# Bucketed attention and a gated Fourier projection on one core: interleaving the two, keeping x on chip, and rewriting four inner pieces

## The chip, the cores and the metric

The kernel runs on one core of one Trainium2 chip. The metric is the device time of one execution in microseconds (us). TensorE is called PE below, VectorE DVE, ScalarE ACT, GpSimd POOL and SyncE SP, as the profile calls them. One run of the kernel before (902.01 us) was slow, and the ratios leave it out. A ratio is the mean time of one kernel's fast runs over that of the other's fast runs of the same rounds, so it is not quite the ratio of the medians that are quoted.

Some terms. PSUM is the memory that matmuls write to, in banks; copying a result out of it is an eviction. A lone pair is a pair of heads in attention that runs with no projection beside it. DFT is the Fourier transform as a product with a table.

## The reference, cut to what matters

Four batches, eight heads, 768 positions, 64 values per head. A query sees only the keys whose six sign bits equal its own. The result, as a matrix x of 768 x 512 per batch, is projected to x1, x2 and x3; x2 is convolved with a filter by way of a Fourier transform, the three are multiplied, and the product is projected again.

```python
q_bits = (einsum('bhsd,dk->bhsk', q, proj) > 0)          # 6 bits; k_bits likewise
mask = q_bucket[:, :, :, None] == k_bucket[:, :, None, :]
scores = where(mask, scale * q @ k.T, -1e9)
attn = exp(scores - max); attn = attn / (sum(attn) + 1e-9)
x = (attn @ v) -> (batch, seq, 512)

x1, x2, x3 = split(x @ w_proj, 3)                        # w_proj 512 x 1536
x2_conv = irfft(rfft(x2) * rfft(filter_fft))             # over the 768 positions
out = (x1 * x2_conv * x3) @ w_out
```

## The kernel before

It does all attention first, sends x to DRAM, then loads tables and weights, then does four projections. In attention the bucket match is a 64-wide table row: signs `hh`, a matmul with a code table (`yps`), two passes of ACT, and the result lies as rows 64 to 127 beside q and k.

```python
tz = ...; zps = matmul(projpad, tz)                       # sign projections, fp32
nc.vector.tensor_scalar(hh[0:70, :], zps[0:70, :], 0.0, None, ALU.is_gt)
nc.tensor.matmul(yps[0:64, 0:512], code_sb[0:6, :], hh[0:6, 0:512])   # ... 4 of them
nc.scalar.activation(prA[HD:P, :], yps[0:HD, :], AF.Relu, bias=..., scale=sc)
...
for jt in range(NCH):                                     # head_front
    stp = pp.tile([P, SEQ], FP32, tag="ps", name="stp")   # two matmuls, then
    nc.scalar.activation(ptj, stp, AF.Exp, bias=negbump_sb, scale=1.0)
...                                                       # pv: 14 matmuls
nc.scalar.copy(t32, pv[0:HD, :])
nc.vector.tensor_tensor(t32, t32, pv[HD:P, :], ALU.add)
nc.vector.tensor_copy(lall[k32 : k32 + 1, :], pv[96:97, :])   # one head's divisors
...
nc.vector.reciprocal(rall, lall)                          # once per four heads
... rhia, rloa = high and low part; rb = matmul(sel128_sb, rhia) + ...  # broadcast
nc.vector.tensor_tensor(u32, t32, rb[0:HD, :], ALU.mult)  # head_tail
... xthi, xtlo -> DRAM
```

The projection works through PSUM tiles of four two-bank buffers, with the forward and inverse transform as plain products with 768 x 768 tables (six row blocks each):

```python
for it in range(NCH): ppj = 12 matmuls; nc.vector.tensor_copy(x2t, ppj)
for jp in range(3):   ab = 2 x 6 matmuls with wfh; 4 products and 2 sums on DVE
for ct in range(NF):  cpd = 2 x 6 matmuls with ivh; p1, p3 = 48 matmuls; 3 DVE operations
for tt_ in range(NCH): op_ = 8 matmuls; nc.vector.tensor_scalar_mul(osb, op_, 1.0 / YSCALE)
```

The softmax here doesn't subtract the row's maximum and nothing guards it: scores larger than these inputs give would overflow.

Of the kernel before, what the change touches and what calls it, by code (L numbers as in the profile page):

```python
# [12 lines left out]
BF16 = mybir.dt.bfloat16  # L14
# [3 lines left out]
P = 128  # L18
SEQ = 768
HD = 64  # L20
NCH = SEQ // P
MASK_BUMP = 30.25
DELTA = 1.0e-7
YSCALE = 1024.0

SPLIT_WPROJ = True
SPLIT_FWD = False
SPLIT_INV = False
SPLIT_WOUT = True
SPLIT_HDFT = True  # L30


def _dft_basis():
    N = SEQ
    tt, rr = np.meshgrid(
        np.arange(N, dtype=np.float64), np.arange(N, dtype=np.float64), indexing="ij"
    )
    kk = np.where(rr <= N // 2, rr, rr - N // 2)
    ang = 2.0 * np.pi * tt * kk / N
    return np.where(rr <= N // 2, np.cos(ang), np.sin(ang))  # L40


def _bucket_consts():
    c = np.arange(64)
    bits = ((c[None, :] >> np.arange(6)[:, None]) & 1).astype(np.float64)
    return 2.0 * bits - 1.0, bits.sum(0)


def _hilo(x):
    hi = x.astype(np.float16)  # L50
    lo = (x - hi.astype(np.float64)).astype(np.float16)
    return hi, lo


@with_exitstack
def kernel(
# [17 lines left out]
    WF64 = _dft_basis()  # L74
    wf_hi, wf_lo = _hilo(WF64)
    wft_hi, wft_lo = _hilo(np.ascontiguousarray(WF64.T))
    wfhi_d = nc.inline_tensor(wf_hi, name="wfhi")
    wflo_d = nc.inline_tensor(wf_lo, name="wflo")
    wfthi_d = nc.inline_tensor(wft_hi, name="wfthi")
    wftlo_d = nc.inline_tensor(wft_lo, name="wftlo")  # L80
    eye_dram = nc.inline_tensor(np.eye(P, dtype=np.float32), name="eye128")

    code_np, pc_np = _bucket_consts()
    code_t = np.zeros((P, 64), dtype=np.float16)
    code_t[0:6, :] = code_np
    code_t[64:70, :] = code_np
    code_dram = nc.inline_tensor(code_t, name="ohcode")
    bias_q = np.zeros((P, 1), dtype=np.float32)
    bias_q[0:64, 0] = MASK_BUMP * (1.0 - pc_np)
    bias_q[64:128, 0] = MASK_BUMP * (1.0 - pc_np)  # L90
    bias_k = np.zeros((P, 1), dtype=np.float32)
    bias_k[0:64, 0] = 1.0 - pc_np
    bias_k[64:128, 0] = 1.0 - pc_np
    biasq_dram = nc.inline_tensor(bias_q, name="biasq")
    biask_dram = nc.inline_tensor(bias_k, name="biask")
    wcol = np.full((P, 3), 2.0 / SEQ, dtype=np.float32)
    wcol[0, 0] = 1.0 / SEQ
    wcol_dram = nc.inline_tensor(wcol, name="wcol")
    import ml_dtypes
    sel = np.zeros((P, 64), dtype=np.float64)  # L100
    sel[0::32, :] = 1.0
    sel128_dram = nc.inline_tensor(sel.astype(ml_dtypes.bfloat16), name="sel128")
    d32 = np.zeros((P, 1), dtype=np.float32)
    d32[32, 0] = 1.0
    d32_dram = nc.inline_tensor(d32, name="d32")

    cp = ctx.enter_context(tc.tile_pool(name="consts", bufs=1))
    pp = ctx.enter_context(tc.tile_pool(name="psm", bufs=4, space=bass.MemoryType.PSUM))
    drp = ctx.enter_context(tc.tile_pool(name="drs", bufs=1, space=bass.MemoryType.DRAM))

    ident = cp.tile([P, P], FP32, name="ident")
    nc.sync.dma_start(ident, eye_dram.ap())
    code_sb = cp.tile([P, 64], FP16, name="code_sb")
    nc.sync.dma_start(code_sb, code_dram.ap())
    biasq_sb = cp.tile([P, 1], FP32, name="biasq_sb")
    nc.sync.dma_start(biasq_sb, biasq_dram.ap())
    biask_sb = cp.tile([P, 1], FP32, name="biask_sb")
    nc.sync.dma_start(biask_sb, biask_dram.ap())
    wcol_sb = cp.tile([P, 3], FP32, name="wcol_sb")
    nc.sync.dma_start(wcol_sb, wcol_dram.ap())  # L120
    sel128_sb = cp.tile([P, 64], BF16, name="sel128_sb")
    nc.sync.dma_start(sel128_sb, sel128_dram.ap())
    projpad = cp.tile([P, 70], FP32, name="projpad")
    nc.vector.memset(projpad, 0.0)
    nc.sync.dma_start(projpad[0:HD, 0:6], proj)
    nc.sync.dma_start(projpad[HD:P, 64:70], proj)
    eps_sb = cp.tile([P, SEQ], BF16, name="eps_sb")
    nc.vector.memset(eps_sb, DELTA)
    negbump_sb = cp.tile([P, 1], FP32, name="negbump_sb")
    nc.vector.memset(negbump_sb, -MASK_BUMP)  # L130
    zero_sb = cp.tile([P, 1], FP32, name="zero_sb")
    nc.vector.memset(zero_sb, 0.0)
    d32_sb = cp.tile([P, 1], FP32, name="d32_sb")
    nc.sync.dma_start(d32_sb, d32_dram.ap())

    xhi_dr = drp.tile([NBAT, NF, P, SEQ], FP16, name="xhi_dr")
    xlo_dr = drp.tile([NBAT, NF, P, SEQ], FP16, name="xlo_dr")

    GRP = 4
    with (  # L140
        tc.tile_pool(name="prime", bufs=26) as prime_p,
        tc.tile_pool(name="qn", bufs=8) as qnp,
        tc.tile_pool(name="qz", bufs=2) as qzp,
        tc.tile_pool(name="hb", bufs=2) as hbp,
        tc.tile_pool(name="pt", bufs=19) as ptp,
        tc.tile_pool(name="vp", bufs=6) as vpp,
        tc.tile_pool(name="grp", bufs=3) as grpp,
        tc.tile_pool(name="ux", bufs=6) as uxp,
    ):
        qpr = {}  # L150
        kpr = {}

        def prep_chunk(b, pr, which):
            hA, hB = 2 * pr, 2 * pr + 1
            if True:
                tensor = q if which == "q" else k
                natA = qnp.tile([P, NCH, HD], FP32, tag="qn", name="natA")
                nc.sync.dma_start(
                    natA, tensor[b, hA].rearrange("(c p) d -> p c d", p=P)
                )  # L160
                natB = qnp.tile([P, NCH, HD], FP32, tag="qn", name="natB")
                nc.sync.dma_start(
                    natB, tensor[b, hB].rearrange("(c p) d -> p c d", p=P)
                )
                tpsA = pp.tile([HD, SEQ], FP32, tag="ps", name=f"tpsA_{which}")
                tpsB = pp.tile([HD, SEQ], FP32, tag="ps", name=f"tpsB_{which}")
                for c in range(NCH):
                    nc.tensor.transpose(tpsA[0:HD, ts(c, P)], natA[:, c, :], ident)  # L168
                    nc.tensor.transpose(tpsB[0:HD, ts(c, P)], natB[:, c, :], ident)
                tz = qzp.tile([P, SEQ], FP32, tag="qz", name="tz")  # L170
                nc.vector.tensor_copy(tz[0:HD, :], tpsA)  # L171
                nc.vector.tensor_copy(tz[HD:P, :], tpsB)  # L172
                prA = prime_p.tile([P, SEQ], FP16, tag="prime", name="prA")
                prB = prime_p.tile([P, SEQ], FP16, tag="prime", name="prB")
                scl = 0.125 if which == "q" else 1.0
                nc.scalar.mul(prA[0:HD, :], tpsA, scl)
                nc.scalar.mul(prB[0:HD, :], tpsB, scl)
                zps = pp.tile([70, SEQ], FP32, tag="ps", name=f"zps_{which}")
                nc.tensor.matmul(zps[:, 0:512], projpad, tz[:, 0:512])  # L179
                nc.tensor.matmul(zps[:, 512:SEQ], projpad, tz[:, 512:SEQ])  # L180
                hh = hbp.tile([P, SEQ], FP16, tag="hb", name="hh")
                nc.vector.tensor_scalar(hh[0:70, :], zps[0:70, :], 0.0, None, ALU.is_gt)  # L182
                yps = pp.tile([P, SEQ], FP32, tag="ps", name=f"yps_{which}")
                nc.tensor.matmul(yps[0:64, 0:512], code_sb[0:6, :], hh[0:6, 0:512])
                nc.tensor.matmul(yps[0:64, 512:SEQ], code_sb[0:6, :], hh[0:6, 512:SEQ])
                nc.tensor.matmul(yps[64:P, 0:512], code_sb[64:70, :], hh[64:70, 0:512])
                nc.tensor.matmul(  # L187
                    yps[64:P, 512:SEQ], code_sb[64:70, :], hh[64:70, 512:SEQ]
                )
                bias_sb = biasq_sb if which == "q" else biask_sb  # L190
                sc = MASK_BUMP if which == "q" else 1.0
                nc.scalar.activation(  # L192
                    prA[HD:P, :], yps[0:HD, :], AF.Relu, bias=bias_sb[0:HD], scale=sc
                )
                nc.scalar.activation(
                    prB[HD:P, :], yps[HD:P, :], AF.Relu, bias=bias_sb[HD:P], scale=sc
                )
                if which == "q":
                    qpr[(b, hA)], qpr[(b, hB)] = prA, prB
                else:  # L200
                    kpr[(b, hA)], kpr[(b, hB)] = prA, prB

        def v_prefetch(b, h):
# [10 lines left out]
            )  # L214
            return vpr

        def head_front(b, h, lall, vpr, filler=None):
            k32 = 32 * (h % GRP)
            ptl = []
            for jt in range(NCH):  # L220
# [311 lines left out]
```

## Time and profile before

| | before |
|---|---|
| median of 4 runs beside the changed kernel | 890.69 us (888.58 to 896.31) |
| attention (0 to 558 us), one pair of heads | 34.2 us (half of 68.3 us per four heads; 20.2 us in the last batch, which prepares no next q and k) |
| tables, weights, filter transform (558 to 594.7 us) | 36.7 us |
| projection, per batch | 72.9 us, four times |

First the page of the kernel before: busy time by engine, then tenths of busy time in 40 slices of the span (22.3 us each), and the granted PE clock in tenths.

```profile
span 891.1 us, 8416 instructions
PE 644.7 (72%) x3256; PEld 319.7 (36%) x3256; DVE 444.8 (50%) x515; ACT 294.7 (33%) x361; POOL 56.9 (6%) x138
...
PE   4666746746646747647647482299999999999997
...
POOL 0022002002002001001112000100000000000000
PEclk9989977976985985985998786599999999999999
...
```

The PE row splits in two. Up to slice 24 it is at 4 to 8 tenths, then at 2 for two slices (the end of attention, then the loading of tables); from slice 27 to 39 it stands at 9 (90% or more). POOL is nearly idle throughout. The view of windows gives the same in numbers; its columns are window, length, busy time of each engine with its instructions, mean granted clock, DMA share and GB/s. First four heads of attention, then one projection:

```profile
core 0: us, PE busy (x) PEld busy (x) DVE busy (x) ACT busy (x) POOL busy (x), PEclk, DMA share, GB/s
187.00:256.00 69.00, 41.70 (x200) 19.61 (x200) 37.53 (x41) 36.73 (x45) 6.55 (x16) 0.83 0.20 46
594.70:667.60 72.90, 72.90 (x398) 38.40 (x396) 36.20 (x51) 0.00 (x0) 0.00 (x0) 1.00 0.11 37
```

In 69 us of attention no engine is full (PE 41.7 us, DVE 37.5, ACT 36.7). In the projection PE is busy all 72.9 us at full clock. So it looks as if in attention engines wait for each other in turn. The chain of waits of the kernel before, in order of time (start, us, what), shows its longest link, once per four heads:

```profile
187.50 0.97 DVE lall L247
...
188.49 4.96 DVE rall L297
...
194.37 0.94 DVE rloa L301
...
195.35 0.64 PE rb L261 x2
...
200.35 1.00 DVE xtlo L275 x2
```

From `lall` to `xtlo` more than 13 us go by in which PE has under 2 us of the chain's work. In the groups (busy us, mean ns, idle before) the wide reciprocal and the one-row copy stand out:

```profile
L297 DVE RECIPROCAL rall<-lall 128x768 f32<-128x768 f32 x8 | 39.6, 4953 | 0.3
...
L247 DVE COPY lall<-pv 1x768 f32<-1x768 f32 x32 | 30.7, 961 | 0.4
```

The copy of one row of 768 values takes 961 ns. In the chain above, the last head's copy stands at its head, at 187.50.

### The profile page before, as it was taken

What the parts mean: (1) busy time and instruction counts of PE and PEld (TensorE: products, weight loads), DVE (VectorE), ACT (ScalarE), POOL (GpSimd) and SP (SyncE); (2) the same over time, 40 slices, a digit from 0 to 9 for tenths busy, and PEclk for the clock granted to TensorE, in tenths of its full rate; (3) what the DMA queues carried; (4) which work ended last, traced back from release to release, by engine and by line L of the source; (5) the groups of instructions that cost most, each with busy time, mean ns of one, the idle gap of its engine ahead of it and who ended that gap; (6) DMA issues with size and microseconds to landing.
All of it is one profiled execution on the core that took longest, in us unless ns stands there. A gap on an engine that the chain in (4) does not pass through costs nothing.

```text
span 891.1 us, 8416 instructions
## 1 busy us (share of the span) xinstructions
PE 644.7 (72%) x3256; PEld 319.7 (36%) x3256; DVE 444.8 (50%) x515; ACT 294.7 (33%) x361; POOL 56.9 (6%) x138
## 2 busy tenths in 40 slices
PE   4666746746646747647647482299999999999997
PEld 2333313313322323322323231044554554554553
DVE  3333465365465365456457657476334533623633
ACT  2447734734734744743756471000000000000000
POOL 0022002002002001001112000100000000000000
PEclk9989977976985985985998786599999999999999
DMA  5242103103102202202101016920030011001001
GB/s 102 57 94 62 34 17 78 42 18 80 45 18 71 54 18 71 54 18 71 36 1 36 1 35 210 288 99 0 1 118 24 1 48 60 1 1 71 1 1 71
DMA packets 94263, 46.92 MB, mean 53 GB/s; under 512 B 78736, under 2 KB 90128, under 8 KB 94224
## 3 DMA queue, kind: packets, MB, share of 16 engines
q1 hardware_dynamic: 93360, 45.60, 19.1%
q0 software_dynamic: 864, 0.79, 0.5%
q8 instruction: 26, 0.43, 0.2%
q14 instruction: 13, 0.11, 0.0%
HBM read 34.58 MB, written 12.58 MB: 53 GB/s over the span
## 4 chain that ended last, share of the span: by engine, by line
PE 58%; DVE 24%; ACT 7%; issue 6%; DMA 3%; SPq 1%; POOL 0%; POOLq 0%; ACTq 0%; DVEq 0%
PE pv L240 8%; PE x1ps L476 7%; PE x3ps L476 7%; PE wprojB L416 7%; ACT ptj L229 5%; DVE rall L297 4%; PE wout L496 4%; PE idft L458 4%; PE fdft L432 3%; DVE hh L182 3%; DVE tz L172 3%; DVE tz L171 3%; PE zps_q L179 3%; DVE xtlo L275 2%; PE zps_k L179 2%
## 5 line engine op out<-in xcount | busy, mean ns | idle before, releaser
L229 ACT ACTIVATE ptj<-stp,negbump_sb 128x768 f16<-128x768 f32 x192 | 158.2, 906 | 29.5 <-PE stp L225 27.9
L240 PE MATMUL pv<-ptj,vpr 128*128 128x256 f16 (+1 forms) x384 | 81.7, 353 | 0.4
L255 PE MATMUL rb<-rhia,sel_sb 32*64 32x512 bf16 (+1 forms) x64 | 15.2, 516 | 69.6 <-ACT rhia L299 69.6
L222 PE MATMUL stp<-prA 128*128 128x512 f16 x96 | 43.4, 464 | 18.8 <-ACT ptj L229 13.0
L240 PEld LDWEIGHTS <-vpr 128*128 128x128 f16 x384 | 40.1, 104 | 34.6 <-issue 13.3
L179 PE MATMUL zps_q<-tz,projpad 128*70 128x512 f32 x32 | 22.8, 802 | 37.8 <-DVE tz L172 37.8
L222 PE MATMUL stp<-prB 128*128 128x512 f16 x96 | 33.9, 378 | 18.1 <-ACT ptj L229 18.1
L297 DVE RECIPROCAL rall<-lall 128x768 f32<-128x768 f32 x8 | 39.6, 4953 | 0.3
L420 DVE CAST x2tile<-wprojB 128x512 f16<-128x512 f32 x24 | 16.5, 690 | 40.1 <-PE wprojB L416 40.1
L179 PE MATMUL zps_k<-tz,projpad 128*70 128x512 f32 x32 | 17.8, 639 | 23.3 <-DVE tz L172 23.3
L182 DVE TENSOR_SCALAR hh<-zps_q 70x768 f16<-70x768 f32 x16 | 15.3, 954 | 35.2 <-PE zps_q L180 35.2
L255 PEld LDWEIGHTS <-sel_sb 32*64 32x64 bf16 x64 | 4.7, 135 | 78.0 <-issue 78.0
L168 PE MATMUL tpsA_q<-ident,natA 128*64 128x128 f32 x96 | 24.6, 333 | 10.3 <-DMA natA<-in_q_dram 8.3
L225 PE MATMUL stp<-prA 128*128 128x256 f16 x96 | 31.9, 332 | 0.0
L247 DVE COPY lall<-pv 1x768 f32<-1x768 f32 x32 | 30.7, 961 | 0.4
L192 ACT ACTIVATE prA<-yps_q,biasq_sb 64x768 f16<-64x768 f32 x16 | 14.3, 894 | 49.0 <-PE yps_q L187 49.0
L171 DVE COPY tz<-tpsA_q 64x768 f32<-64x768 f32 x16 | 15.2, 948 | 29.0 <-PE tpsA_q L168 29.0
L171 DVE COPY tz<-tpsA_k 64x768 f32<-64x768 f32 x16 | 15.2, 950 | 28.5 <-PE tpsA_k L168 28.5
L182 DVE TENSOR_SCALAR hh<-zps_k 70x768 f16<-70x768 f32 x16 | 15.3, 954 | 27.7 <-PE zps_k L180 27.7
L192 ACT ACTIVATE prA<-yps_k,biask_sb 64x768 f16<-64x768 f32 x16 | 14.3, 894 | 39.4 <-PE yps_k L187 39.4
L500 DVE TENSOR_SCALAR osb<-wout 128x512 f32<-128x512 f32 x24 | 16.4, 692 | 21.1 <-DMA out_dram<-osb 10.8
L416 PEld LDWEIGHTS <-xh 128*128 128x128 f16 x192 | 18.8, 98 | 22.6
(622 smaller groups left out, 1514.5 us busy)
## 6 DMA issues: line engine op xcount, KB each, us to landing
out_dram<-osb SPq DMA_DIRECT2D x24, 256.0 KB, 2.1
natA<-in_q_dram SPq DMA_DIRECT2D x16, 192.0 KB, 2.5
natB<-in_q_dram SPq DMA_DIRECT2D x16, 192.0 KB, 2.7
natA<-in_k_dram SPq DMA_DIRECT2D x16, 192.0 KB, 2.7
natB<-in_k_dram SPq DMA_DIRECT2D x16, 192.0 KB, 2.8
xhi_dr<-xthi SPq DMA_DIRECT2D x32, 96.0 KB, 2.2
xlo_dr<-xtlo SPq DMA_DIRECT2D x32, 96.0 KB, 2.1
xh<-xhi_dr SPq DMA_DIRECT2D x16, 192.0 KB, 3.7
```

The source lines that it names most:

```text
L171: nc.vector.tensor_copy(tz[0:HD, :], tpsA)
L179: nc.tensor.matmul(zps[:, 0:512], projpad, tz[:, 0:512])
L182: nc.vector.tensor_scalar(hh[0:70, :], zps[0:70, :], 0.0, None, ALU.is_gt)
L222: nc.tensor.matmul(stp[:, 0:512], kpr[(b, h)][:, ts(jt, P)], qpr[(b, h)][:, 0:512])
L225: nc.tensor.matmul(stp[:, 512:SEQ], kpr[(b, h)][:, ts(jt, P)], qpr[(b, h)][:, 512:SEQ])
L229: nc.scalar.activation(ptj, stp, AF.Exp, bias=negbump_sb, scale=1.0)
L240: nc.tensor.matmul(pv[:, lo_c:hi_c], vpr[:, jc, :], ptl[jc][:, lo_c:hi_c], start=False, stop=(jc == NCH - 1),)
L297: nc.vector.reciprocal(rall, lall)
L416: nc.tensor.matmul(ppj, lh, rh, start=(i == 0), stop=(i == len(terms) - 1))
L458: nc.tensor.matmul(cpd[:, lo_c:hi_c], lh, rh, start=(i == 0), stop=(i == len(terms) - 1),)
L476: nc.tensor.matmul(dest[:, lo_c:hi_c], lh, rh, start=(i == 0), stop=(i == len(terms) - 1),)
L496: nc.tensor.matmul(op_, lh, rh, start=(i == 0), stop=(i == len(terms) - 1))
```

## The change

The intent: let PE do the projection of batch b while batch b+1 is in attention, so that neither half's waits leave PE idle, and shorten the attention chain. Its parts:

- **Order.** The loop runs the four pairs of batch b, then writes the projection of batch b-1; a scheduler decides the order on each engine. PSUM is split: 2 x 2 banks for scores, 2 for `pv`, 2 single banks (`psW`) for everything else.
- **x on chip.** The 16 pair tiles `xh`, `xl` stay in SBUF.
- **Divisors by DMA.** The sums' row goes to a 128 x 12 tile by DMA (`lt`), the reciprocal is short there, and two DMAs bring it back over DRAM to all rows of `R`.
- **Half-bit rows.** Six rows of (bit - 1/2) directly beside q and k; no table matmul, no ACT.
- **Folded transforms.** Sums and differences of thirds cut the products: per batch 16,384 fewer matmul columns.
- **Work moved.** The scaling of q and k, casts of weights and the lows of x go to POOL.

```diff
-                nc.vector.tensor_scalar(hh[0:70, :], zps[0:70, :], 0.0, None, ALU.is_gt)
-                ... yps: 4 matmuls; 2 x nc.scalar.activation(prA/prB ..., AF.Relu, ...)
-                nc.scalar.mul(prA[0:HD, :], tpsA, scl)
+        nc.gpsimd.tensor_scalar(row[(which, 0)][0:HD, :], tz[0:HD, :], scl, None, ALU.mult)
+        nc.gpsimd.tensor_scalar(row[(which, 1)][HD:P, :], tz[HD:P, :], scl, None, ALU.mult)
+            nc.vector.tensor_scalar(
+                row[(which, 0)][64:70, cs], zps[64:70, :], 0.0, 0.5, ALU.is_gt, ALU.subtract
+            )                                      # and the same for rows 0 to 5
 ...
-            nc.vector.tensor_copy(lall[k32 : k32 + 1, :], pv[96:97, :])
-                nc.vector.reciprocal(rall, lall)
-                ... rhia, rloa, rb matmuls, x to DRAM and back
+        nc.scalar.copy(S[rows, :], pv[HD:P, :])
+        nc.vector.scalar_tensor_tensor(T[rows, :], in0=S[rows, :], scalar=mask[rows, :], ...)
+            nc.sync.dma_start(lt[:, par, :], S[r0 : r0 + 1, 0:SEQ])
+        nc.vector.reciprocal(rl, rl)
+        nc.sync.dma_start(rdr.rearrange("h (p c) -> p h c", p=P), rl)
+            nc.sync.dma_start(R[...], rdr[par : par + 1, :].to_broadcast([HD, SEQ]))
+        nc.vector.scalar_tensor_tensor(
+            U, in0=T[:, 0:SEQ], scalar=vsd, op0=ALU.add, in1=R, op1=ALU.mult)
+        nc.vector.tensor_copy(th, U)
+        nc.gpsimd.tensor_tensor(tl, U, th, ALU.subtract)
 ...
+    for pr in range(NPAIR):                        # batch 0
+        pair(pr); prep_pair(pr + 2)
+        if pr == 1: setup(stg)                     # tables, weights, filter transform
+        for b in range(1, NBAT):
+            for pr in range(NPAIR):
+                pair(g); prep_pair(g + 2)
+            phase_b(b - 1, fbp)                    # projection of the batch before
+        phase_b(NBAT - 1, fbp)
 ... (forward and inverse transform by thirds, filter transform likewise: cut)
```

## The prediction

> **What bounds it now.** The page splits at 558 us. Before it (attention) no engine is full: the table of windows gives PE 58 to 65%, DVE 53 to 56%, ACT 51 to 59%. The chain of waits is serial: transposes, tz, zps, hh, yps, prA, then pv; and once per four heads lall, the 4.95 us reciprocal, rhia, rb, u32, xtlo. Four heads take 68.3 us (lall to lall), 40.4 us in the last batch. From 558 to 594 us tables and weights load. From 594 us to the end PE is 100% busy at granted clock 1.00: 72.9 us per batch (wprojB to wprojB).
>
> **What the change does, costed from the trace.** Warm matmuls of 512 columns start 215 ns apart, 768 columns cost 0.33 us; the Trainium skill's "TensorE: Matmul & The Clock Gate" (Back-to-back issue gap) says columns/2.4 + 2.5 ns, and the trace agrees.
>
> *Attention.* Removed: yps and its four ACT passes per pair, lall copies (0.96 us a head), wide reciprocals, rb matmuls, eps matmuls, the trip of x through DRAM. Added: a DMA round trip of the divisors (three landings, each about 2.1 to 2.8 us, off PE), POOL work. Estimates per head pair: PE 24 x 0.33 + zps 2 x 1.5 + 12 transposes x 0.22 = 13.4 us; ACT 12 x 0.80 + 2 x 0.8 = 11.2; DVE about 10.3; POOL about 10 (cast of 384 columns 0.50, two-input 192 columns 0.55). So the pair becomes bound by PE and by the coupling through small PSUM pools (2+1+2 tiles); I expect 16 us against 34.2 before.
>
> *Projection.* Columns per batch fall from 172,032 to 155,648: 66 us of PE instead of 72.9. Folding saves only 7 us: x1/x3 (73,728 columns) stay. New stalls: only two one-bank PSUM tiles, twelve DVE evictions of 0.69 us in the forward DFT (8.3 us against 4.3 us of PE), then subtracts on POOL (about 1.5 us each): +4 us where attention fills in, +9 to 11 us for the last two batches.
>
> *Overlap.* The order of instructions shows little true interleaving: projection b meets roughly one pair of batch b+1, the other three pairs and the last projection run alone. So overlap removes little.
>
> *Setup.* Now beside pairs 1 to 3, but about 40 us of casts and subtracts move to POOL ahead of the v tiles that pairs 2 and 3 need: about 25 us of waiting.
>
> **Sum.** 13 lone pairs x 16 = 208; 3 overlapped pairs x 14 = 43; projections 70 + 70 + 75 + 77 = 292; filter DFT 9; setup wait 25; start 15; tail 5: 597, rounded to 600 us. Nearly all is on the critical path.
>
> Predicted 600 us, 8 in 10 within 555 to 650. Faster by over 2%: 0.97; within 2%: 0.02; slower by over 2%: 0.01.
>
> **What would show it.** Pair period (exp groups) 15 to 17 us in batch 1; PE clock near 1.0 throughout except around 45 to 90 us; PE busy over 85% after 120 us; last projection alone 74 to 80 us, with a gap at the first idrq; POOL tables ending near 90 us with pv waiting for vpr; R landings 7 to 9 us after S.
>
> **What would make it wrong.** POOL slower (one subtract took 1.25 instead of 0.55 us before): pairs at 18 to 20 us. DVE waiting in order for R, holding up tz and so PE. PE gaps that bring the slow clock back (mean 0.885 now), doubling PE time in attention. On the good side, pairs at 14 us and hidden setup: 550 us.

## The result, and the profile after

The changed kernel took **592.32 us** (median of 4, 591.20 to 594.10) against 890.69 us: a ratio of 0.6648, 95% interval 0.6621 to 0.6675. The predicted 600 us lies 1.3% above that.

The page after, the same lines (a slice is now 14.7 us):

```profile
span 589.2 us, 7097 instructions
PE 507.2 (86%) x2552; PEld 259.6 (44%) x2552; DVE 293.6 (50%) x527; ACT 213.7 (36%) x273; POOL 283.7 (48%) x274
...
PE   4993955977989879999699879999997899987997
...
POOL 7999998997886331019876240018613200013000
PEclk9996777999899999999979899999998999998999
...
```

From the eighth slice on PE is at 7 tenths or more in all but one, POOL is busy 92.4 of the first 100 us, and POOL's busy time is five times that of before. The clock drops in slices 4 to 7, where PE waits for POOL. The windows of the second 50 us, of the four lone pairs of batch 1 (from the first exp of one pair to that of the next), and of the last projection, which runs alone:

```profile
core 0: us, PE busy (x) PEld busy (x) DVE busy (x) ACT busy (x) POOL busy (x), PEclk, DMA share, GB/s
50.00:100.00 50.00, 30.97 (x121) 14.30 (x120) 26.26 (x40) 15.04 (x18) 48.15 (x39) 0.74 0.42 115
112.74:126.13 13.39, 12.69 (x70) 6.95 (x69) 8.49 (x16) 11.59 (x15) 12.69 (x16) 1.00 0.70 177
126.13:146.34 20.21, 14.49 (x69) 7.25 (x67) 13.24 (x22) 11.70 (x15) 17.01 (x16) 0.92 0.36 80
146.34:161.94 15.60, 14.31 (x70) 7.67 (x69) 10.57 (x20) 11.86 (x14) 12.96 (x13) 0.89 0.42 101
161.94:178.19 16.25, 13.04 (x69) 6.63 (x67) 10.89 (x20) 11.67 (x15) 13.40 (x13) 1.00 0.42 100
500.04:577.03 76.99, 69.24 (x357) 35.12 (x356) 27.62 (x52) 6.24 (x12) 7.47 (x6) 0.98 0.06 21
```

The parts of the sum that the prediction gave can be read off the trace, by the starts of the first exp of a pair and of the first output eviction (`osb`) of a projection:

| part | predicted | measured | how read |
|---|---|---|---|
| start | 15 | 16.3 | first exp |
| batch 0 with setup | 64 + 9 + 25 = 98 | 96.5 | 16.25 to 112.74 |
| batch 1, four lone pairs | 64 | 65.5 | 112.74 to 178.19 |
| the rest: 5 lone and 3 overlapped pairs, 4 projections, tail | 80 + 43 + 292 + 5 = 420 | 411.0 | 178.19 to the span's end |
| of that, the last projection | 77 | 77.0 | osb at 500.04 to 577.03 |

So the total held, and held in each part that was read. Whether the reasons held is another question, and three lines of the profile after bear on it: the first and the third do not fit the reasons that the sum rests on, the second fits them in part. First, POOL's scaling of 64 rows takes 2.13 us (and a two-input operation over 128 rows 1.64 us):

```profile
L195 POOL TENSOR_SCALAR pr_k_0_96<-tz 64x768 f16<-64x768 f32 x6 | 12.8, 2128 | 0.5
```

```profile
L289 POOL TENSOR_TENSOR xl<-U,xh 128x768 f16<-128x768 f32 x16 | 26.3, 1642 | 76.2 <-DVE xh L287 75.9
...
L283 DVE SCALAR_TENSOR_TENSOR U<-T,vsd,R 128x768 f32<-128x768 f32 x16 | 19.0, 1189 | 25.4 <-DMA R<-rdr 25.4
```

Per pair POOL does four scalings, 3.4 us for v (two times 0.12 + 0.50 + 0.55 + 0.54) and one `xl`: 4 x 2.13 + 3.4 + 1.64 = 13.6 us, about as much as PE's 12.7 to 14.5 us. Second, in the chain of waits from 14 to 79 us there is nearly nothing but POOL, as in this stretch:

```profile
59.21 2.73 POOL pr_k_0_95 L194
...
62.01 2.14 POOL pr_k_0_96 L195
...
64.22 1.64 POOL xl L289
...
69.00 3.10 POOL wpl_605 L342
...
74.24 0.78 POOL vpr L215
75.02 3.05 POOL wpl_611 L342
...
79.13 3.80 PE pv L245 x12
```

The `vpr` (the v tile) of the third pair stands behind scalings, `xl` and weight casts in POOL's list, and `pv` waits for it. The weight casts there were foreseen; the scalings had not been priced. Third, in the lone pairs the chain goes through the divisors' trip:

```profile
134.82 2.42 DMA rdr<-rl
...
137.79 5.64 DMA R<-rdr
...
143.51 1.22 DVE U L283
...
144.76 0.55 DVE pr_q_1_99 L203
...
147.07 0.60 PE tps_k L190 x3
```

`U` waits for `R` and holds DVE; behind it in DVE's list stands a small row of the next pair (`pr_q`), for which a transpose on PE waits. The same chain in the view of waits (us in all, times, longest), for all pairs:

```profile
DVE U L283 <- DMA R<-rdr: 25.4, 11, 4.1
```

### The profile page after: what moved, and what is told of

Same layout as the page of the kernel before. It is cut to its first block, busy times and chain, and to the rows that moved or that the text cites. A ratio compares the mean times of both kernels' runs of the same rounds, so it can differ in the third digit from the quotient of the medians.

```text
span 589.2 us, 7097 instructions
## 1 busy us (share of the span) xinstructions
PE 507.2 (86%) x2552; PEld 259.6 (44%) x2552; DVE 293.6 (50%) x527; ACT 213.7 (36%) x273; POOL 283.7 (48%) x274
## 4 chain that ended last, share of the span: by engine, by line
PE 46%; POOL 24%; DMA 11%; DVE 9%; issue 4%; ACT 3%; SPq 2%; DVEq 0%; ACTq 0%; POOLq 0%
PE wout L398 7%; DMA R<-rdr 5%; PE pv L245 4%; DMA rdr<-rl 4%; PE stp L235 3%; PE x2b L398 2%; PE idrq L398 2%; PE x2c L398 2%; POOL vpr L219 2%; POOL vpr L216 2%; PE zps_k L199 1%; PE zps_q L199 1%; PE x2a L398 1%; POOL vpr L215 1%; DVE U L283 1%
## 5 line engine op out<-in xcount | busy, mean ns | idle before, releaser
L289 POOL TENSOR_TENSOR xl<-U,xh 128x768 f16<-128x768 f32 x16 | 26.3, 1642 | 76.2 <-DVE xh L287 75.9
L245 PEld LDWEIGHTS <-vpr 128*128 128x128 f16 x384 | 38.1, 99 | 47.8 <-issue 13.5
L251 DVE SCALAR_TENSOR_TENSOR T<-S,cst_sb,pv 64x769 f32<-64x769 f32 x32 | 32.3, 1011 | 26.9 <-ACT S L250 26.4
L250 ACT COPY S<-pv 64x769 f32<-64x769 f32 x32 | 25.5, 798 | 40.6 <-PE pv L245 40.4
L190 PE MATMUL tps_k<-cst_sb,nat_k 128*128 128x128 f32 x96 | 17.9, 299 | 23.8 <-DVE pr_q_0_93 L203 15.2
L283 DVE SCALAR_TENSOR_TENSOR U<-T,vsd,R 128x768 f32<-128x768 f32 x16 | 19.0, 1189 | 25.4 <-DMA R<-rdr 25.4
L199 PE MATMUL zps_k<-tz,projpad 128*70 128x384 f32 x64 | 31.6, 599 | 0.0
L199 PE MATMUL zps_q<-tz,projpad 128*70 128x384 f32 x64 | 26.8, 513 | 0.0
L190 PEld LDWEIGHTS tps_k<-cst_sb,nat_k 128*128 128x128 f32 x96 | 11.3, 149 | 34.0 <-issue 20.3
L240 ACT ACTIVATE pt_110<-stp,nmatch 128x768 f16<-128x768 f32 x16 | 14.4, 901 | 24.2 <-PE stp L235 23.9
L240 ACT ACTIVATE pt_120<-stp,nmatch 128x768 f16<-128x768 f32 x16 | 14.4, 898 | 20.7 <-PE stp L235 20.6
L193 DVE COPY tz<-tps_k 128x384 f32<-128x384 f32 x32 | 17.5, 547 | 8.2 <-PE tps_k L190 7.2
L245 PE MATMUL pv<-pt_110,vpr 128*128 128x512 f16 (+1 forms) x32 | 11.0, 370 | 12.3 <-POOL vpr L219 12.1
L240 ACT ACTIVATE pt_114<-stp,nmatch 128x768 f16<-128x768 f32 x16 | 14.4, 901 | 16.7 <-PE stp L235 16.2
L235 PE MATMUL stp<-pr_q_0_92,pr_k_0_95 70*128 70x512 f16 x72 | 19.3, 352 | 1.2 <-ACT pt_110 L240 0.7
```

The source lines that it names most:

```text
L190: nc.tensor.transpose(tps[:, ts(i, P)], nat[:, c3, j].rearrange("p h d -> p (h d)"), ident)
L193: nc.vector.tensor_copy(tz[:, cs], tps)
L199: nc.tensor.matmul(zps, projpad, tz[:, cs])
L235: nc.tensor.matmul(stp[:, lo_c:hi_c], kp[kr, ts(jt, P)], qp[kr, lo_c:hi_c])
L240: nc.scalar.activation(pt[:, 0:SEQ], stp, AF.Exp, bias=nmatch, scale=LSCALE)
L245: nc.tensor.matmul(pv[:, lo_c:hi_c], vpr[:, jt, :], pl[jt][:, lo_c:hi_c], start=(jt == 0), stop=(jt == NCH - 1),)
```

## The experiments

Twelve kernels ran, each in three rounds beside the kernel before. The theory that goes in: the gain is mostly shorter attention; in the lone pairs DVE's wait for `R` binds, in batch 0 POOL does; the projections lose time where the forward transform waits for DVE and POOL. Rivals: the gain is overlap; or folding; or the pairs are bound by PE, as the prediction had it. One caution holds for all of them. A scheduler orders each engine's list by its own idea of durations, so an edit can move instructions that it doesn't name. The kernel before took 890.7 to 892.8 us (medians), so medians of the table can be compared to within 1 or 2 us.

| run | us (median) | ratio to before, 95% |
|---|---|---|
| after | 592.32 | 0.6648 [0.6621, 0.6675] |
| e1_rows_dve | 578.80 | 0.6485 [0.6449, 0.6522] |
| e2_no_trip (wrong result) | 581.09 | 0.6505 [0.6470, 0.6539] |
| e3_setup_act_dve | 585.64 | 0.6553 [0.6518, 0.6587] |
| e4_fenced | 629.10 | 0.7047 [0.7015, 0.7079] |
| e5_late_norm | 590.92 | 0.6628 [0.6614, 0.6641] |
| e6_product_first | 576.38 | 0.6454 [0.6436, 0.6472] |
| e7_fine | 581.68 | 0.6521 [0.6504, 0.6538] |
| e8_all | 536.83 | 0.6022 [0.6005, 0.6039] |
| e9_pinned | 583.88 | 0.6556 [0.6523, 0.6590] |
| e10_all_pinned | 533.62 | 0.5997 [0.5975, 0.6019] |
| e11_unfolded | 598.14 | 0.6718 [0.6693, 0.6742] |
| e12_all_unfolded | 553.91 | 0.6210 [0.6189, 0.6231] |

### e1_rows_dve: the scalings from POOL to DVE

```diff
-        nc.gpsimd.tensor_scalar(row[(which, 0)][0:HD, :], tz[0:HD, :], scl, None, ALU.mult)
-        nc.gpsimd.tensor_scalar(row[(which, 1)][HD:P, :], tz[HD:P, :], scl, None, ALU.mult)
+        nc.vector.tensor_scalar(...)               # both
```

> The four row scalings of a pair (64x768, 2.13 us each on POOL, 136 us in all) go to DVE, where I estimate 0.55 us each from the 0.55 us copies of 384 columns and casts of the trace. Theory A (POOL is what a lone pair and batch 0 wait for: 13.7 us of POOL work per pair, and POOL links in most of the chain from 14 to 131 us): POOL busy falls from 284 to about 150 us, lone pairs from 16.4 to 14 to 15 us, batch 0 (first exp of pair 0 to first exp of pair 4, 96.5 us) to 75 to 82 us; total 550 to 567 us. Theory B (the divisors' round trip through DVE sets the lone pair, POOL is only busy): lone pairs stay at 16 us or grow, since DVE gets 2 us more; total 580 to 600 us.

Measured: correct, 578.80 us (577.09 to 582.56), between the two theories' ranges. POOL's busy time falls from 283.7 to 151.1 us, DVE's rises from 293.6 to 338.5: the 64 scalings cost about 2.1 us each on POOL and 0.7 us each on DVE. The whole gain lies in batch 0: the last copy of `S` (each head's last ACT operation) of its fourth pair comes at 98.1 us instead of 111.9. The lone pairs of batch 1 stay at 16.4 us (98.1 to 163.8), although POOL is busy only 20.0 us of those 65.7. (By copies of `S`, the kernel after has 16.0 us, from 111.9 to 175.9; by first exps, as above, 16.4.) So POOL binds batch 0, and does not alone bind the lone pairs. What held them here is not shown: `U` waited only 4.6 us for `R` in the four, and DVE was busy 50.8 us.

### e2_no_trip: nobody waits for R (wrong on purpose)

```diff
-            U, in0=T[:, 0:SEQ], scalar=vsd, op0=ALU.add, in1=R, op1=ALU.mult
+            U, in0=T[:, 0:SEQ], scalar=0.0625, op0=ALU.mult, in1=S[:, 0:SEQ], op1=ALU.min
```

> Wrong result on purpose: U no longer reads the divisors, so nothing waits for the DMA round trip; all its transfers still run. Theory B (DVE waits in order for R: 25 us in total, 8 us of it in batch 1, and PE then waits for tz and the bit rows): lone pairs fall from 16.4 to about 14.4 us, total 565 to 577 us. Theory A (POOL): under 6 us gained, total 586 to 594 us.

Measured: 581.09 us (578.57 to 583.37), between the two theories' ranges, the result wrong. The trip itself still runs (its DMAs are all in the trace); only the wait is gone. The lone pairs take 14.4 us (S copies at 110.6 and 168.2, four pairs), batch 0 is nearly unchanged (110.6 against 111.9). So the wait for `R`, and not PE's work, made up the 1.6 to 2.0 us by which a lone pair was longer in the kernel after (16.0 by copies of `S`, 16.4 by first exps). PE's work did not change (52.8 us busy in those 57.6, 54.4 in the kernel after); POOL is now busy 54.8 of them.

### e3_setup_act_dve: weight casts to ACT, their subtractions to DVE

```diff
-            nc.gpsimd.tensor_copy(th, w32)
+            nc.scalar.copy(th, w32)
-            nc.gpsimd.tensor_tensor(tl, w32, th, ALU.subtract)
+            nc.vector.tensor_tensor(tl, w32, th, ALU.subtract)
 ...          (w_out and the filter's sums likewise)
```

> The casts and subtractions of tables and weights (about 38 us on POOL) go to ACT and DVE. My predicted setup wait of 25 us: batch 0 falls from 96.5 to 70 to 78 us, the step from pair 2 to pair 3 from 40 to about 20 us; total 565 to 575 us. Rival: the loads themselves (7.5 MB beside q, k, v) or the row scaling hold batch 0; then under 8 us are gained, total 584 to 594 us.

Measured: correct, 585.64 us (584.61 to 588.18). The total lies in the rival's range, though batch 0 moved as the theory had it, if by less: the gain did not last. Batch 0 ends 16 us earlier (96.0 against 111.9), and batch 1 then takes 10.7 us longer (to 170.6). So the setup's POOL work cost 16 us there, and most of the gain was given back in the next stage. In batch 1 `U` waited 13.0 us for `R`, 9.7 at the longest, against 8.2 and 3.7 in the kernel after, so the divisors' trip can be at most about half of the 10.7 us. The rest, and why the trip got longer, was not settled.

### e4_fenced: no overlap

```diff
+            tc.no_sync_barrier()                   # the scheduler moves nothing across
             phase_b(b - 1, fbp)
+            tc.no_sync_barrier()
```

> A fence for the scheduler before and after each projection: attention and projection no longer interleave on any engine, all else as it was. My prediction said that overlap removes little: then three pairs lose about 2.5 us each and three projections about 4 us each in fill, total 600 to 615 us. Rival, the interleaving that the change is named for carries the gain: total above 640 us.

Measured: correct, 629.10 us (628.60 to 631.13), between the theory's range and the rival's, and 36.8 us over the kernel after: 12.3 us for each of the three overlapped projections. The lone pairs are as before the fence (16.2 us, 16.0 in the kernel after). Between the profiled runs the span grows by 39.8 us (629.0 against 589.2): PE is busy 12.6 us more (519.8 against 507.2, at a mean clock of 0.938 instead of 0.949) and idle 27.2 us more. So overlap, with the preparation of the next pairs that the fence also holds back, is worth 37 us; 262 of the 298 us of gain (890.69 - 629.10 of 890.69 - 592.32) are there without it.

### e5_late_norm: U written one pair later (a miss)

```diff
     for par in range(2): head(g, par, vs[par], S, T)
+    if late is not None: late()                    # vsd, U, xh, xl of pair g-1
```

> The normalisation of a pair (vsd, U, x high and low) is written after the heads of the next pair, so that it stands later in DVE's order and its divisors have landed; result unchanged. If the waits for R that ended in the run without the trip (581.1 us, lone pairs 14.4 us) were the cause, this recovers most of it: lone pairs 14.4 to 15.2 us, idle before U under 8 us instead of 25, total 578 to 584 us. Rival: what helped there was only that U stood elsewhere or read other data; then total 589 to 595 us.

Measured: correct, 590.92 us (590.13 to 592.32), no gain. This does not speak against the trip: the scheduler had put `U` back nearly where it was, and `U` still waited 23.7 us for `R` in 11 places. The edit had not made the case that it was to test. e9 repeats it.

### e6_product_first: x1 * x3 between the transform's parts

```diff
             for zone in range(2):
                 ps = ...; group(ps, fwd_terms(...)); 2 DVE products
+                next(fill)                         # one 12-matmul group of x1 or x3
 ...
-                        m_ = cv * px ; y_ = m_ * YSCALE * px      (per half, after the inverse)
+            y_ = cv * YSCALE * m13[ct]             # m13 = x1 * x3, made before
```

The reason is in the timeline of the kernel after, in the last projection. Each line is a matmul group on PE with, in brackets, how long PE had stood idle and what ended it:

```profile
526.78 0.59 PE L398 MATMUL fdft<-fp,f1h 128*128 128x512 f16 x2 [0.64 <-DVE u__4600 L438]
...
530.74 0.59 PE L398 MATMUL fdft<-fp,f1h 128*128 128x512 f16 x2 [1.74 <-DVE u__4620 L438]
...
534.69 0.27 PE L398 MATMUL ida<-ia,z__4609 128*128 128x256 f16 x1 [1.74 <-DVE u__4642 L438]
...
536.70 0.61 PE L398 MATMUL idrq<-irq,z__4653 128*128 128x512 f16 x1 [0.58 <-POOL z__4653 L442]
```

From 524.2 to 537.1 us, 12.9 us, the twenty matmuls of the forward transform (4.3 us at 215 ns each), and a few more, are all that PE does.

> The product of x1 and x3 for two column tiles is made between the zones of the forward DFT, instead of after the inverse; same arithmetic but for the order of the product. In the lone last projection (77.0 us from one first output tile to the next) PE has 4.3 us of work in a stretch of about 13 us from the last x2c matmul to the first x13 group. If this is a wait for DVE and POOL that other PE work can fill: last projection 69 to 71 us, the one before it the same, the overlapped ones 2 to 4 us shorter, total 570 to 578 us. Rival: the stretch is latency of the folded transform that comes back at the inverse; total above 586 us.

Measured: correct, 576.38 us (573.98 to 577.08), 16 us less. The last projection, osb to osb, takes 71.5 us (492.26 to 563.75) instead of 77.0. So 5.5 us of waiting in the last projection, and 4 us per projection on average (15.9 over four), was real and is filled by PE work that depends on none of it.

### e7_fine: the projection in quarters, one after each pair

```diff
             pair(g); prep_pair(g + 2)
+            if pr == 0: work = phase_b(b - 1, fbp)
+            next(work, None)                       # a quarter of the projection
```

> Each projection is cut in four and a quarter is written after each pair of the next batch, instead of all of it after the fourth pair. If overlap is worth filling PE's idle time wherever both sides are there (the fence cost 12 us per overlapped projection), now all twelve pairs of batches 1 to 3 are filled: total 560 to 575 us. Rival: the two shared one-bank PSUM tiles make the preparation of q and k wait behind projection groups, so pairs are late and nothing is gained: 588 to 610 us.

Measured: correct, 581.68 us (580.11 to 582.91), 10.6 us less than after, between the theory's range and the rival's. Written after each pair, the projection fills some of the gaps, and not as many as expected. Why it did not start there before was not tested; the reading is that the two single PSUM banks are taken in program order.

### e8_all: e3, e5, e6, e7 together, and the k scalings on ACT

```diff
+        if which == "k": nc.scalar.mul(row[...], tz[...], scl)     # ACT
         else: nc.gpsimd.tensor_scalar(...)                         # q stays on POOL
 ...     and the edits of e3, e5, e6, e7
```

> Late normalisation, product first, projections in quarters, k row scalings on ACT, table casts on ACT and their subtractions on DVE, together; correct result. If the four limits are separate stretches of the same time line, gains add: 12 + 15 + 20 + 14 us, some of it shared: total 530 to 550 us. If they only trade places (each removal gives the next one the critical path, as where setup left POOL and batch 1 then grew by 10 us): 555 to 575 us.

Measured: correct, 536.83 us (535.58 to 539.02), ratio 0.6022. PE is busy 488.3 us, 91% of the span, at a clock of 0.987; POOL is down to 190.5 us. The whole saving of 55 us is larger than the savings of e3, e5, e6 and e7 alone added up (6.7 + 1.4 + 15.9 + 10.6 = 35 us); the 13.5 us that e1 gains with all four scalings off POOL would cover most of the other 20.9, but only the k scalings moved here, and they were not run alone.

### e9_pinned: e5 done properly

```diff
+            tc.keep_in_program_order(nc.vector.tensor_scalar(vsd, ...))   # stands behind the
+            tc.keep_in_program_order(nc.vector.scalar_tensor_tensor(U, ...))  # next pair's T
```

> As e5_late_norm, but U and the small product ahead of it are also pinned in program order, so that in the list that VectorE works through U of a pair stands behind T of the second head of the next pair (this was read from the built kernel: in e5 the scheduler had left U where it was). The answer stays right. Theory: in batches where U waits on VectorE for R, the tile that comes by way of DRAM, everything behind U in VectorE's list waits too. Then the waits of U for R fall from 25.4 us in all to under 5 us, the lone pairs of batch 1 go from 16.4 us to between 14.4 and 15.2 us each, as in e2_no_trip, and the time is 578 to 584 us. Rival: U's wait only fills time in which VectorE has nothing to do that anyone waits for, and e2 gained for another reason (it also drops the traffic and the reciprocal): then the lone pairs stay near 16.4 us and the time is 589 to 595 us.

Measured: correct, 583.88 us (580.45 to 586.92). The waits fell as the theory had it:

```profile
DVE U L291 <- DMA R<-rdr: 4.9, 3, 3.2
```

and three of the four lone pairs last 13.5 us, the third 18.3, together 14.7 on average (S copies at 110.42 and 169.12). Windows of the second to fourth:

```profile
123.88:137.33 13.45, 12.55 (x70) 6.85 (x69) 10.15 (x20) 11.65 (x15) 12.75 (x13) 1.00 0.32 71
137.33:155.65 18.32, 14.53 (x70) 7.34 (x69) 10.38 (x20) 11.88 (x15) 17.45 (x19) 0.91 0.47 111
155.65:169.12 13.47, 12.78 (x70) 6.85 (x69) 10.71 (x20) 11.65 (x14) 12.77 (x14) 1.00 0.41 87
```

The time is at the upper end of what the theory gave and clear of the rival. (The rival's text says that e2 drops the traffic and the reciprocal; it doesn't, as the trace of e2 shows.) So two ways of not waiting for `R`, one with a right result, bring the lone pair from 16.4 (16.0 by copies of `S`) to 14.4 or 14.7 us. What binds then is not shown by a run. In a pair of 13.5 us POOL is busy 12.8 us and PE 12.6 to 12.8. In the view of waits of these four pairs POOL waits for nothing and PE for 5.1 us, and in the one long pair POOL is busy 17.5 of 18.3 us, PE 14.5: this speaks for POOL, with PE just behind it.

### e10_all_pinned: the best version

> e8_all with the same pin. In e8 U still waits for R 33.3 us in all on VectorE, 12 times. If these waits hold TensorE, whose busy share in e8 is 91 per cent, the time is 525 to 533 us; if TensorE has enough other work in its list while VectorE waits, it stays at 535 to 539 us.

The edit is e9's pin on e8. Measured: correct, 533.62 us (532.97 to 534.70), ratio 0.5997 [0.5975, 0.6019], the best of all kernels here. `U` waited for `R` once (6.3 us) instead of 12 times, but the ratios' intervals of e8 and e10 overlap, and 533.6 lies between what the two theories gave. So the pin's worth here can't be told from nothing: where PE has other work in its list, DVE's wait costs little or nothing. The page:

```profile
PE 487.1 (92%) x2552; PEld 251.7 (47%) x2552; DVE 295.0 (56%) x523; ACT 261.9 (49%) x345; POOL 194.2 (37%) x222
...
PEclk9998599999999999999999999999999999999999
```

### e11_unfolded: the folding undone, all else as after

```diff
-    s_, p_, d_ = sums and differences of thirds (x2 and filter); fdft with f0h, f1h (2 and 4 blocks)
-    ida, idrq, then 5 DVE/ACT operations to recombine
+    x2t = 6 copies; fdft with wfh (6 blocks); idft with iv (6 blocks) and one ACT copy
```

> The kernel after with the folding by thirds undone and all else as it is: forward DFT by six row blocks of the full matrix, inverse DFT by six row blocks, filter transformed the same way. It removes the sums, differences and recombinations on VectorE and GpSimd, and adds 16,384 matmul columns per batch, which at 215 ns per 512 columns is 6.9 us of TensorE per batch, and about 7 us in the setup. Theory: in the projection TensorE is what binds, so the folding is worth nearly its whole TensorE time: 612 to 625 us. Rival: the folded stages wait for the sums and recombinations of the other engines, so the folding buys little: 603 us or less.

Measured: correct, 598.14 us (596.38 to 599.86): only 5.8 us over the kernel after, inside the rival's range. PE is busy 529.9 us, 22.7 us more.

In the last projection the trace shows where part of it hid: 79.4 us osb to osb (504.06 to 583.46) with PE busy 74.9 of them, against 77.0 with 69.2. The folded form has 5.7 us less PE work and stands idle 3.3 us more. So the folding paid one quarter of what it saved on PE. The added columns alone would be 34 us, an estimate (5 x 16,384 at 215 ns per 512); PE's busy time rose by less, and the mean clock is 0.968 against 0.949 in the kernel after. So some of the folding's saving also went into a lower clock, which no run took apart.

### e12_all_unfolded: the folding undone in e10

> e10_all_pinned with the folding by thirds undone, as e11_unfolded undid it in the kernel after (the filter's casts on VectorE, two buffers shared to make room). In e11 TensorE was busy 22.7 us more than in after, and the time rose only about 6 us. Theory: after's folded projection stood still for other engines (13 us for 4.3 us of matmuls ahead of the first x1 group), and that ate what the folding saves; e10 has product groups in those stretches, TensorE is busy 92 per cent there, so here the folding pays nearly all that it saves: 550 to 560 us. Rival: the matmuls that the folding adds or saves hide elsewhere (throttle, scheduler), so undoing it costs again about 6 us: 537 to 543 us.

Measured: correct, 553.91 us (552.70 to 554.29), 20.3 us over e10, as the theory had it.

```profile
PE 513.7 (93%) x2744; PEld 271.9 (49%) x2744; DVE 259.0 (47%) x453; ACT 257.8 (47%) x333; POOL 185.9 (34%) x222
...
PEclk9999999999999999999999999999999999999999
```

PE is busy 513.7 us instead of 487.1. So the same edit is worth 20.3 us where PE is fed, and 5.8 us where the stage waits for DVE and POOL. The mean clock, 1.000 against 0.987, is on the side of the slower kernel, so a lower clock does not explain these 20.3 us.

## Why the prediction was right

**Right: what bounds before, and that nearly all of the gain is on the critical path.** A lone pair fell from 34.2 to 16.4 us (16 predicted). Sixteen pairs at 17.8 us less are 285 us, an estimate of the largest term; e4, without overlap, shows 262 us of gain in all. How the 17.8 us divide among the half-bit rows, the divisors by DMA, the split of PSUM and x on chip is not shown: no run undid one of them alone.

**Right: the stalls of the projection.** 77.0 us for the last one, against 77 predicted and 72.9 before. e6 filled most of them, and got 71.5 us. That the figure is met exactly is luck: PE was busy 69.2 us (66 predicted) and idle 7.8 (11 predicted).

**Right: what setup would cost.** Batch 0 took 96.5 us (98 predicted). e3 shows the named cause, the casts on POOL ahead of the v tiles: 16 us come back when they leave POOL. e1 shows a second one that was not named: 14 us come back when the scalings leave it. Against 36.7 us in the open before, hiding the setup gains only about 6 us net (96.5 - 65.5 = 31 us are its price beside batch 0), by subtraction, not by a run.

**Right in size, wrong in reason: "the pair becomes bound by PE and by the coupling through small PSUM pools".** PE was busy 12.7 to 14.5 us in a lone pair, 13.4 predicted. But e2 and e9 took 1.3 to 2.0 us (by copies of `S`, by first exps) off the pair and left PE's work alone. What made it longer was DVE, in order, waiting for `R`; behind that POOL and PE are about equally full (e9). No run tested the PSUM pools. The text named the wait for `R` and a slower POOL as what could make it wrong; they did occur, and were worth less than the spread.

**Mis-sized: "POOL about 10".** It was 13.6 us per pair. The scaling of 64 x 768 values on POOL had no duration in the trace before; it took 2.13 us.

**Mis-sized: "R landings 7 to 9 us after S".** In the chain shown above, the second S copy of the pair ends at 126.1 us (125.31 + 0.80) and `R` has landed at 143.4: 17 us. Three landings are 2.1 (median of `lt`) + 2.4 + 5.6 = 10.1 us of that. The rest is mostly queueing in two in-order lists: the divisors' arithmetic starts at 130.7 on DVE and ends at 132.0, and `rdr` is issued at 134.8, behind loads of a later pair's k in the SP queue. The view of that queue's waits, 110 to 180 us:

```profile
SPq L176 <- POOL vpr L219: 14.0, 3, 6.1
...
```

L176 is the load of q and k. It waits for a buffer that POOL frees when the v tile is made (L219), and the `rdr` and `R` transfers are issued behind it. So POOL's slowness reached DVE by way of the DMA queue. This is read from the trace; no run took that queue apart.

**Mis-sized: "So overlap removes little".** The sum implied some 18 us (three pairs at 14 instead of 16, two projections at 70 instead of 76). e4 measured 36.8. The order of instructions showed a projection meeting about one pair only, and that was taken for little. In the fenced kernel PE idled 27.2 us more and was busy 12.6 us more, at a lower mean clock; how the two share the causes was not taken apart.

**Right on PE, and its price was in the sum: "Folding saves only 7 us" per batch.** The four projections stand in the sum with 292 us, against 4 x 72.9 = 291.6 before: what folding saves on PE was spent again on new stalls. e11 agrees that little is left, 5.8 us of time for 22.7 us of PE, setup included.

**Luck in the total.** Without overlap the sum would have been 597 + 18 = 615 us, and the fenced kernel took 629.1. So the sum left out 14 us of cost and 19 us of overlap, which all but cancel. Where the 14 us lie is not shown.

## What to carry to other kernels

Here, work moved off a busy engine came back as waiting, since the new engine was slower and its list held something urgent: price it on the engine that receives it, and look at what stands behind it. An instruction that waits for a DMA round trip belongs behind the next piece's work in an in-order list, and one must check in the built kernel that the scheduler left it there. Saving PE work is worth its PE time only where PE is fed: the same folding gave 5.8 us in one kernel and 20.3 us in the other, so try to fill the stage's waits first.

## What the Trainium skill lacked or had wrong

- **"GPSIMD Engine Reference", 3.1 Elementwise — side-by-side cycle accounting**, has GpSimd 1.96 times slower than VectorE for a two-input fp32 add, and about 2.6 cycles per element because two inputs share a read port, 1.03 cycles being the bound for bodies with few operations. Here the one-input scaling of 64 x 768 fp32 to fp16 took 2.13 us on POOL (2.8 ns a column), more per column than the two-input `xl` at 1.64 us over 128 rows (2.1 ns a column), and 3 to 4 times what it takes on VectorE in e1 (median 0.55 us, mean 0.70). A cast of 384 columns took 0.50 us (1.3 ns a column). A table of scalings with an output cast is lacking.
- **"TensorE: Matmul & The Clock Gate", Architectural detail**, says that the queues of ScalarE and VectorE are strictly first in, first out. This is no lack; the traces agree: in the timeline of the kernel after DVE stood idle 3.67 us ahead of the `U` at 143.51, and the next row started 0.03 us after its end; with `U` placed later the waits fell from 25.4 to 4.9 us (e9).
- **"DMA: Bandwidth & Descriptors", Anatomy of one DMA — SWDGE (gpsimd) path**, gives about 2 us of fixed cost (for the software path; these go through the hardware queue). `lt` (3 KB) landed in 2.1 us, which agrees; but `rdr` (6 KB) took a median of 2.8 and `R` (192 KB) 3.4 us, up to 5.9, and the whole trip 17 us, for the queueing. What an in-order issuing queue costs when a transfer stands behind an unrelated load's wait (14.0 us of such waits in 70) is not in the section.
- **"TensorE: Matmul & The Clock Gate", Back-to-back issue gap**, gives two figures for 512 columns: 131 ns apart, measured in a sustained stream with weight loads, and about 216 ns by a formula for an isolated matmul. In the last projection of the kernel after, a stream with a weight load for each matmul, they start 215 ns apart at full clock. So the formula fits here and the sustained figure does not.
- **"VectorE: DVE Perf Modes", Why `tensor_reduce` can't reduce along partition axis**, says that each partition is an independent lane. The traces show what follows for narrow operations: a copy of 1 x 768 takes 961 ns, of 64 x 768 950 ns, and the six-row operations of the half bits 0.55 us for 384 columns, as much as a copy of 128 x 384. No line there warns of one-row work.
